# Making the x[128] rows of ten tiles once and loading them by DMA, and a block-diagonal S in the Fourier stage

## The chip, the cores and the metric

One NeuronCore of a Trainium2 chip runs the whole program. The metric is the device time of one execution in microseconds (us); times given are medians of several runs. Engines: TensorE (PE, matrix products, with PEld its weight loads), VectorE (DVE), ScalarE (ACT), GpSimd (POOL), and SyncE (SP), which here only issues DMAs.

## The reference

The input x is 2 x 3008 x 256, f32. It is Fourier transformed along the sequence and along the features, the real part is kept, and the 6016 tokens go through two feed-forward layers with 2048 hidden features:

```python
X = np.fft.fft(np.fft.fft(x, axis=1), axis=2).real        # 2 x 3008 x 256 -> 6016 x 256
h = X @ w_in;   y = (np.maximum(h, 0.0) ** 2) @ w_out      # first layer
h = y @ w_in2;  P = a0 + a1*h + a2*h*h + a3*h*h*h
Q = 1 + abs(b0)*abs(h) + abs(b1)*h*h
out = (P / (Q + 1e-6)) @ w_out2                            # second layer
```

## The kernel before, in words

**The transform.** 3008 = 64 x 47. A start-up part multiplies x by the length-47 matrix and leaves the result in the SBUF tile U. The rest is done per token tile: *D* (f_d, line 490) multiplies two units of U (128 columns) by the matrices of the feature transform, which leaves 2 x 129 columns in PSUM: a cosine part and a sine part of 64 + 64 features each, and in each part a last column for feature 128 (x[128]). *v* (f_v, line 498) copies that to SBUF on ACT. *S* (f_s, line 512) does the length-64 transform: v is the stationary operand, a constant of sines and cosines (rcs) the moving one. f_eh (line 528) rounds the result to the matmul format on ACT (the high part, tile x1h, and X0 with the rows for x[128]); f_el (line 544) makes the low part by a subtraction on DVE (line 547), and the low part of row 64 of X0 (line 549).

**One job** is D, v, S, f_eh and f_el for two units, that is 128 columns of the tile's transformed input. In v of before, each unit's cosine and sine halves have to end up on all 128 partitions, so there are four copies of 64 partitions x 129 (line 509; job 0 of tile 0 is special, with one copy, line 502). S then has four matmuls in a job: for each of the two units one with 128 moving columns (line 523) and one with 64 (line 524). The second one has feature 128 of v, broadcast to 128 stationary columns, so that every row of its result is x[128]; it goes to X0. All these are f32 matmuls, which the trace shows as two passes each, each pass with a weight load of its own.

**The layers.** There are 12 tiles: tile 0 has 3 units, the others 4 (two jobs each; 47 units and 24 jobs, of which job 0 of tile 0 is special). Tokens k and -k share their products: the first layer's matmuls (h1, lines 630 to 633 for the DIRECT tiles 0 and 1, lines 648 and 650 for the others) work on half of a tile's columns. Each product of f32 accuracy is three matmuls of high and low parts; the contribution of feature 128 is a seventh matmul with w0 as the weights and X0 as the moving operand (line 650; line 631 in the DIRECT tiles). w0 is zero but in rows 0, 32 and 64, which hold the high, low and high part of that row of w_in; X0's rows 0, 32 and 64 must hold x[128]'s high, high and low part. o1 and o2 (line 674) are the output matmuls of the layers, h2 (line 617) the second layer's input matmul; ACT, DVE and POOL do the polynomials between them. Layer 2 of a tile runs beside layer 1 of the next one, and the jobs of a tile beside layer 1 of the tile before it.

**The order.** No engine's order is written out. Every operation is entered with `add(key, engine, cost, place, fn, needs, take, give, ...)`: an estimated cost, a due place, what it needs, and which buffers it takes and gives back. Queues.run (line 63) goes through them as a list scheduler with a clock per engine: of everything that can start earliest it takes the one with the smallest place. The order found this way is the program order of every engine. So a changed cost or a dropped operation can change the order of others. Engines run their queues in order on the chip.

**Start-up.** The weights of both layers are 64-bit floats and are loaded, converted and split on ACT and DVE while tiles 0 and 1 run. The U units of tiles 2 to 11 are spilled to DRAM (udram) and read back per tile (fd). Between the jobs of tile 0, TensorE also runs two groups of six matmuls on a tile of zeros (`hot`, line 286) which nothing reads.

Of the kernel before, what the change touches and what calls it, by code (L numbers as in the profile page):

```python
# [9 lines left out]
F32 = mybir.dt.float32  # L10
# [26 lines left out]
LAG1, LAG2, M2_AT, M2_SPAN = 1.23, 4.02, 1.04, 15.75  # L37
F_AT, F_STEP, F_GAP, F_GAP0 = 1.05, 3.59, 2.15, 0.4
# [119 lines left out]
def body(ctx: ExitStack, tc: tile.TileContext, x0, xf, w1i, w1o, w2i, w2o, a_in, b_in,  # L158
# [14 lines left out]
    rcs = cd_t[:, 258:514].rearrange("p (u c n) -> p u c n", u=2, c=2)  # L173
# [3 lines left out]
    a0, a1, a2, b0 = (ab[:, i:i + 1] for i in (0, 1, 2, 4))  # L177
    udram = dr.tile([128, 2, 94 * 32], F32, name="udram")
# [95 lines left out]

    hot_t = stp.tile([128, 128], F32, name="hot_t")
# [234 lines left out]


    def f_s(t, k, tag):
        v = FU.pop((t, k, "v"))
        f = ps(tag, [128, 512])
        FU[t, k] = p, r = f[:, 0:256].rearrange("p (c n) -> p c n", c=2), f[:, 256:384]
        if t + k == 0:
            nc.tensor.matmul(p[:, 0, :], v[:, 0:128], r0c, start=True, stop=True)
            nc.tensor.matmul(p[:, 1, :], v[:, 129:257], r0s, start=True, stop=True)
            nc.tensor.matmul(r, v[:, 128:129].to_broadcast([66, 128]), r0c, start=True, stop=True)
        else:  # L520
            for u in range(2):
                cols = slice(u * 64, u * 64 + 64)
                nc.tensor.matmul(p[:, :, cols], v[:, u, 0:128], rcs[:, u], start=True, stop=True)
                nc.tensor.matmul(r[:, cols], v[:, u, 128:129].to_broadcast([128, 128]), rcs[:, u, 0], start=True, stop=True)

    def f_eh(t, k, i):
        if i == 0:
            X1[t] = [sb("x1" + part, [128, 2, NMAX // 2], F32R) for part in "hl"]  # L530
            X0[t] = sb("x0", [128, NMAX // 2], F32R)
# [3 lines left out]
        nc.scalar.activation(out=X0[t][:, cols], in_=r, func=ACTF.Copy)  # L535
# [8 lines left out]
    def f_el(t, k, i):  # L544
        cols = slice(i * 128, i * 128 + 128)
        p, r = FU.pop((t, k))
        nc.vector.tensor_tensor(out=X1[t][1][:, :, cols], in0=p, in1=f32(X1[t][0][:, :, cols]), op=ALU.subtract)
        x = X0[t][64:65, cols]
        nc.vector.tensor_tensor(out=x, in0=r[64:65], in1=f32(x), op=ALU.subtract)

    for t in range(T):
# [5 lines left out]
        for i, k in enumerate(jobs):  # L557
# [9 lines left out]
            single = t + k == 0  # L567
            for part in range(1 if single else 2):
                add(("fv", t, k, part), "ACT", act(258, True) if single else 2 * act(129, True), place,
                    lambda k=key, p=part: f_v(*k, p), needs=[("fm",) + key] + ([("fv", t, k, 0)] if part else []),  # L570
                    give=(ft if t == 0 else ft[0],) if part or single else (), lat=0.2)
            add(("fs",) + key, "PE", 2 * mm4(128) + 2 * mm4(64), place + gap,
                lambda k=key, g=st: f_s(*k, bank(g)), needs=[("fv", t, k, 0 if single else 1)], take=(st,), give=("v",), lat=0.2)
            add(("fe",) + key, "ACT", act(256, True) + act(128, True), place + gap, lambda k=key, i=i: f_eh(*k, i),
                needs=[("fs",) + key], take=("x1h", "x1l", "x0") if k == 0 else (), after=[("fe", t, 0)] if k else [])
            add(("ff",) + key, "DVE", dve(256) + dve(128), place + gap, lambda k=key, i=i: f_el(*k, i),
                needs=[("fe",) + key], give=(st if t == 0 else st[0],), lat=0.2)
# [7 lines left out]
        needs=[k for k in queues.by_key if k[0] == "spill"] + [k for k in queues.by_key if k[0] in ("fm", "fs") and k[1] < 2]  # L585
# [245 lines left out]
    for t, j in ORDER1:  # L831
        for first, gs in (GROUPS1[t][j],):
# [8 lines left out]
                needs=[k for k in queues.by_key if k[0] in ("ff", "fn") and k[1] == t] + ["w0"] + [("W", 1, i) for i in chunks],  # L841
# [84 lines left out]
def _consts():  # L926
# [99 lines left out]
```

## Time and profile before

| what | value |
|---|---|
| median of 3 runs | 1083.6 us (1082.31 to 1086.79) |
| profiled execution, its own time | 1083.8 us |
| its span in the trace | 1082.0 us |
| granted TensorE clock, mean over the span | 0.997 |
| PE / PEld busy | 1048.7 us (97%) / 987.8 us (91%) |
| DVE / ACT busy | 1008.0 us (93%) / 985.9 us (91%) |
| POOL busy | 488.8 us (45%) |

A row of instruction groups gives the source line, the engine, the operation, output <- input, shapes and count, then the busy time, the mean in ns of one, and the idle time before them. In a timeline, a row is one instruction or a run of equal ones: start, length, engine, line. A matmul's length is latency, and consecutive ones overlap: what one costs TensorE is read from the starts of its successors. A clock of 1.00 is 2.4 GHz; the other level is 1.2 GHz.

### The profile page before, as it was taken

What the parts mean: (1) busy time and instruction counts of PE and PEld (TensorE: products, weight loads), DVE (VectorE), ACT (ScalarE), POOL (GpSimd) and SP (SyncE); (2) the same over time, 40 slices, a digit from 0 to 9 for tenths busy, and PEclk for the clock granted to TensorE, in tenths of its full rate; (3) what the DMA queues carried; (4) which work ended last, traced back from release to release, by engine and by line L of the source; (5) the groups of instructions that cost most, each with busy time, mean ns of one, the idle gap of its engine ahead of it and who ended that gap; (6) DMA issues with size and microseconds to landing.
All of it is one profiled execution on the core that took longest, in us unless ns stands there. A gap on an engine that the chain in (4) does not pass through costs nothing.

```text
span 1082.0 us, 21256 instructions
## 1 busy us (share of the span) xinstructions
PE 1048.7 (97%) x7670; PEld 987.8 (91%) x7670; DVE 1008.0 (93%) x1808; ACT 985.9 (91%) x2008; POOL 488.8 (45%) x371
## 2 busy tenths in 40 slices
PE   9999989999999999999999999999999999999996
PEld 9899979899999999989899989999989999999885
DVE  6999999999899999999899899999899999889998
ACT  3888989999989999989999999999999999999997
POOL 0000025454454555445555545545545545545476
PEclk9999999999999999999999999999999999999989
DMA  9654400000000000000000000000000000000000
GB/s 337 205 205 128 137 1 2 25 1 11 10 12 11 11 11 11 2 20 11 2 21 11 1 21 11 2 21 12 1 21 10 2 11 11 2 11 11 1 11 20
DMA packets 26821, 36.81 MB, mean 34 GB/s; under 512 B 2299, under 2 KB 19325, under 8 KB 26717
## 3 DMA queue, kind: packets, MB, share of 16 engines
q1 hardware_dynamic: 26605, 35.07, 9.6%
q8 instruction: 61, 1.00, 0.4%
q14 instruction: 43, 0.35, 0.1%
q10 hardware_dynamic: 112, 0.39, 0.1%
HBM read 26.65 MB, written 8.78 MB: 33 GB/s over the span
## 4 chain that ended last, share of the span: by engine, by line
PE 43%; ACT 30%; DVE 17%; issue 6%; DMA 1%; POOL 1%; POOLq 0%; SPq 0%; ACTq 0%; DVEq 0%
PE o2a L674 11%; PE p L617 7%; PE o1a L674 5%; PE o1b L674 5%; ACT y L764 4%; PE p L648 4%; ACT t L741 3%; ACT g L703 3%; ACT y L768 3%; ACT g L709 3%; ACT u L751 3%; PE o2b L617 3%; DVE p L787 3%; ACT u L736 3%; DVE u L747 2%
## 5 line engine op out<-in xcount | busy, mean ns | idle before, releaser
L798 POOL TENSOR_TENSOR g<-t,y 128x512 fp32r<-128x512 f32 (+1 forms) x181 | 248.1, 1371 | 420.0 <-DVE t L794 334.5
L718 POOL TENSOR_TENSOR g<-g,g 128x512 fp32r<-128x512 f32 x160 | 211.2, 1320 | 153.5 <-ACT g L713 101.8
L674 PE MATMUL o2a<-g,w2hi 128*128 128x256 f32 (+1 forms) x1440 | 262.6, 283 | 7.9 <-POOL g L798 6.0
L674 PEld LDWEIGHTS o2a<-g,w2hi 128*128 128x128 f32 x1440 | 210.1, 189 | 15.5 <-POOL g L798 8.6
L781 DVE SCALAR_TENSOR_TENSOR g<-t,ab,y 128x512 fp32r<-128x512 f32 (+1 forms) x177 | 137.1, 776 | 11.7 <-ACT y L768 10.9
L674 PE MATMUL o2a<-g,w2lo 128*128 128x256 f32 (+1 forms) x720 | 144.6, 281 | 0.0
L674 PE MATMUL o1a<-g,w1hi 128*128 128x512 f32 x352 | 140.0, 398 | 1.5 <-POOL g L718 1.5
L674 PE MATMUL o1b<-g,w1hi 128*128 128x512 f32 x352 | 138.6, 394 | 0.0
L787 DVE SCALAR_TENSOR_TENSOR p<-u,g 128x512 f32<-128x512 f32 (+1 forms) x176 | 131.3, 746 | 0.7
L794 DVE SCALAR_TENSOR_TENSOR t<-t,ab,p 128x512 f32<-128x512 f32 (+1 forms) x177 | 128.5, 726 | 1.1
L751 ACT ACTIVATE u<-u 128x512 f32<-128x512 f32 (+1 forms) x176 | 109.5, 622 | 14.0 <-DVE u L747 13.3
L617 PE MATMUL p<-x2h,w2hi 128*128 128x256 f32 (+1 forms) x534 | 110.4, 288 | 8.2 <-DVE t L759 3.7
L768 ACT ACTIVATE y<-y 128x512 f32<-128x512 f32 (+1 forms) x185 | 115.3, 624 | 1.6
L764 ACT ACTIVATE y<-u 128x512 f32<-128x512 f32 (+1 forms) x176 | 109.1, 621 | 7.1 <-POOL g L798 3.5
L703 ACT ACTIVATE g<-g 128x512 f32<-128x512 f32 x160 | 101.2, 632 | 15.4 <-DVE g L693 15.1
L747 DVE SCALAR_TENSOR_TENSOR u<-u,ab,p 128x512 f32<-128x512 f32 (+1 forms) x133 | 96.5, 726 | 19.3 <-ACT t L741 18.0
L709 ACT ACTIVATE g<-g 128x512 fp32r<-128x512 f32 (+1 forms) x175 | 109.7, 627 | 3.3 <-PE o1b L674 1.9
L674 PEld LDWEIGHTS o2a<-g,w2lo 128*128 128x128 f32 x720 | 110.7, 189 | 0.0
L713 ACT ACTIVATE g<-g 128x512 f32<-128x512 f32 (+1 forms) x175 | 109.5, 626 | 1.2
L617 PE MATMUL p<-x2h,w2lo 128*128 128x256 f32 (+1 forms) x534 | 107.9, 284 | 0.0
L617 PE MATMUL p<-x2l,w2hi 128*128 128x256 f32 (+1 forms) x534 | 107.8, 284 | 0.0
L693 DVE TENSOR_TENSOR g<-p,bc 128x256 f32<-128x256 f32 x238 | 96.2, 415 | 5.6 <-ACT bc L683 2.3
(261 smaller groups left out, 2862.4 us busy)
## 6 DMA issues: line engine op xcount, KB each, us to landing
g<-in_dram SPq DMA_DIRECT2D x48, 256.0 KB, 3.1
xt<-in_dram SPq DMA_DIRECT2D x15, 384.0 KB, 5.6
out_dram<-os SPq DMA_DIRECT2D x22, 256.0 KB, 2.1
udram<-U SPq DMA_DIRECT2D x4, 640.0 KB, 5.2
ut<-udram SPq DMA_DIRECT2D x10, 256.0 KB, 3.1
x2h<-in_dram SPq DMA_DIRECT2D x8, 256.0 KB, 5.0
x2l<-in_dram SPq DMA_DIRECT2D x8, 256.0 KB, 4.3
xt<-in_dram ACTq DMA_DIRECT2D x1, 384.0 KB, 4.1
```

Source lines behind the costliest of these rows:

```text
L617: nc.tensor.matmul(h[:, c * n:(c + 1) * n], l[:, k, :], r[:, k], start=(q == 0), stop=(q == 5))
L674: nc.tensor.matmul(O[t][e], l[:, e * 128:(e + 1) * 128], r[:, c * n:(c + 1) * n], start=(i == 0 and q == 0 and (e == 0 or not one)), stop= ...
L703: nc.scalar.activation(out=e["g"], in_=e["g"], func=ACTF.Relu)
L709: nc.scalar.activation(out=e["gh"], in_=e["g"], func=ACTF.Square)
L718: eng.tensor_tensor(out=e["gl"], in0=e["g"], in1=f32(e["gh"]), op=ALU.subtract)
L751: nc.scalar.activation(out=w, in_=w, func=ACTF.Abs)
L764: nc.scalar.activation(out=e["z"], in_=e["w"], func=ACTF.Abs_reciprocal_sqrt, bias=Q1)
L768: nc.scalar.activation(out=z, in_=z, func=ACTF.Square)
L781: nc.vector.scalar_tensor_tensor(out=e["gh"], in0=e["t1"], scalar=a0, in1=e["z"], op0=ALU.add, op1=ALU.mult)
L787: nc.vector.scalar_tensor_tensor(out=e["m"], in0=e["w"], scalar=Q1, in1=f32(e["gh"]), op0=ALU.add, op1=ALU.mult)
L794: nc.vector.scalar_tensor_tensor(out=e["t1"], in0=e["t1"], scalar=a0, in1=e["m"], op0=ALU.add, op1=ALU.subtract)
L798: (nc.vector if (t, j) in FIN else nc.gpsimd).tensor_tensor(out=e["gl"], in0=e["t1"], in1=e["z"], op=ALU.mult)
```

## The change

- **S** of the jobs after the first: the moving constant `rcs` becomes two block-diagonal matrices (128 x 128 each: two units in one), so that v keeps the layout that D leaves. One copy of D's result per job does for the four; S has two matmuls of 128 moving columns. In the DIRECT tiles 0 and 1, S keeps a third matmul, of 128 columns, for x[128].
- **x[128] of tiles 2 to 11**: D leaves out its column there (128 moving columns for 130), S its matmuls, f_eh its second copy and f_el its second subtraction.
- **New, once, in start-up**: 20 matmuls with one moving column each (q_mm, one per pair of units, in four groups of five), one ACT copy of the 20 columns (q_copy), one 128-column matmul (q_s), a rounding on ACT (q_hi), a subtraction on DVE (q_lo), and two DMAs from SP to DRAM (q_out).
- **New, per tile from 2 on**: three DMAs from SP that read rows 0, 32 and 64 of X0 from DRAM (q_row). The first-layer matmuls of the tile need them. X0 is one of two constant buffers; the DMAs take the buffer when the first layer of the tile two before has given it back.
- **Removed**: the two `hot` groups of tile 0.

```diff
+Q_AT, Q_STEP = -11.5, 0.5
...
-        nc.tensor.matmul(v[:, :, 64:129], u[:, 0, :], ca, start=True, stop=True)
+        last = 65 if t in DIRECT else 64
+        nc.tensor.matmul(v[:, :, 64:64 + last], u[:, 0, :], ca[:, :, :last], start=True, stop=True)
...
-        a, b = part * 64, 64 - part * 64
-        for o, c in ((a, 0), (b, 129)):
-            nc.scalar.activation(out=v[o:o + 64, part, :], in_=p[a:a + 64, c:c + 129], func=ACTF.Copy)
+        v = FU[t, k, "v"] = sb("v", [128, 258])[:p.shape[0]]
+        if t not in DIRECT:
+            v, p = (x.rearrange("p (b n) -> p b n", b=2)[:, :, 0:128] for x in (v, p))
+        nc.scalar.activation(out=v, in_=p, func=ACTF.Copy)
...
-            for u in range(2):
-                cols = slice(u * 64, u * 64 + 64)
-                nc.tensor.matmul(p[:, :, cols], v[:, u, 0:128], rcs[:, u], start=True, stop=True)
-                nc.tensor.matmul(r[:, cols], v[:, u, 128:129].to_broadcast([128, 128]), rcs[:, u, 0], start=True, stop=True)
+        for c in range(2):
+            nc.tensor.matmul(p[:, c], v[:, c * 129:c * 129 + 128], rcs[:, c], start=True, stop=True)
+        if t in DIRECT:
+            nc.tensor.matmul(r, v[:, 128:129].to_broadcast([128, 128]), rcs[:, 0], start=True, stop=True)
...
-        nc.scalar.activation(out=X0[t][:, cols], in_=r, func=ACTF.Copy)
+        if t in DIRECT:
+            nc.scalar.activation(out=X0[t][:, cols], in_=r, func=ACTF.Copy)
...
+        if t not in DIRECT:
+            return
         x = X0[t][64:65, cols]
         nc.vector.tensor_tensor(out=x, in0=r[64:65], in1=f32(x), op=ALU.subtract)
...
+    def q_mm(i, n):
+        if i == 0:
+            QP["v"] = ps("p3", [128, 512])
+        for k in range(i, i + n):
+            u = sum(TILES[:2]) + 2 * k
+            nc.tensor.matmul(QP["v"][:, k:k + 1], Uf[:, 0, (u - 1) * 64:(u + 1) * 64], ca[:, 0, 64:65], start=True, stop=True)
+    def q_copy():
+        nc.scalar.activation(out=qs, in_=QP["v"][:, 0:20], func=ACTF.Copy)
+    def q_s():
+        QP["q"] = q = ps("p3", [128, 512])[0:20, 0:128]
+        nc.tensor.matmul(q, qs, rcs[:, 0], start=True, stop=True)
+    def q_hi():
+        nc.scalar.activation(out=qh, in_=QP["q"], func=ACTF.Copy)
+    def q_lo():
+        nc.vector.tensor_tensor(out=ql, in0=QP["q"], in1=f32(qh), op=ALU.subtract)
+    def q_row(t):
+        X0[t] = x0t[t % 2]
+        k = (unit0[t] - sum(TILES[:2])) // 2
+        for row, part in ((0, 0), (32, 0), (64, 1)):
+            nc.sync.dma_start(out=f32(X0[t][row:row + 1]), in_=qdram[part:part + 1, k:k + 2].rearrange("o j n -> o (j n)"))
+    def q_out():
+        for part, x in enumerate((qh, ql)):
+            nc.sync.dma_start(out=qdram[part], in_=f32(x))
+    for i in range(0, 20, 5):
+        add(("qm", i), "PE", 5 * 0.22, Q_AT + i / 5 * Q_STEP, lambda i=i: q_mm(i, 5), needs=U_ALL, take=() if i else ("p3",),
+            after=[("qm", i - 5)] if i else [("fv", 0, 0)], lat=0.2)
...
+    for t in range(2, T):
+        add(("q", t), "SP", 0.4, 16 * (t - 1) + F_AT - 6, lambda t=t: q_row(t), take=("x0",), needs=["qd"], lat=DMA_LAT,
+            after=[("q", t - 1)] if t > 2 else [("fe", 1, 0)])
...
-            if t == 0:
-                add(("hot",) + key, "PE", 0.222 * 6, place + gap + 0.1, lambda: hot(6, "p0"), take=("p0",), give=("p0",),
-                    needs=[("fm",) + key])
...
-                needs=[k for k in queues.by_key if k[0] in ("ff", "fn") and k[1] == t] + ["w0"] + [("W", 1, i) for i in chunks],
+                needs=[k for k in queues.by_key if k[0] in ("ff", "fn", "q") and k[1] == t] + ["w0"] + [("W", 1, i) for i in chunks],
...
     rc[32], rs[0], rs[32] = alt, alt, -1.0
-    cc, ss = np.concatenate([rc, 0 * rc], axis=1), np.concatenate([0 * rs, rs], axis=1)
-    rcs = np.concatenate([np.concatenate([cc, ss]), np.concatenate([ss, cc])], axis=1)
+    rcs = np.block([[rc, z2, rs, z2], [z2, rc, z2, rs]])
```

The costs that the planner is given follow: v is one operation with the cost of 256 or 258 elements in place of two, S two 128-column matmuls (three in the DIRECT tiles), f_eh and f_el without their 128-element parts outside the DIRECT tiles.

## Rows read from the trace of the kernel before

**Rows 1.** The page's first part: busy us (share of the span) x instructions.
```profile
PE 1048.7 (97%) x7670; PEld 987.8 (91%) x7670; DVE 1008.0 (93%) x1808; ACT 985.9 (91%) x2008; POOL 488.8 (45%) x371
```
**Rows 2.** Windows: length, busy of PE, PEld, DVE, ACT, POOL, clock, DMA share, GB/s.
```profile
81.00:108.00 27.00, 27.00 (x197) 25.95 (x196) 24.50 (x50) 22.41 (x46) 0.00 (x0) 1.00 0.41 128
...
900.00:1000.00 100.00, 100.00 (x739) 94.65 (x738) 92.19 (x162) 95.99 (x190) 52.91 (x41) 1.00 0.03 9
```
**Rows 3.** Timeline of TensorE: one S of tile 11 and what follows.
```profile
902.30 0.38 PE L523 MATMUL p<-cd_t,v 128*128 128x128 f32 x2
902.52 0.33 PE L524 MATMUL p<-cd_t,v 128*128 128x64 f32 x2
902.69 0.44 PE L523 MATMUL p<-cd_t,v 128*128 128x128 f32 x2
902.96 0.33 PE L524 MATMUL p<-cd_t,v 128*128 128x64 f32 x2
903.11 0.48 PE L617 MATMUL p<-x2h,w2hi 128*128 128x256 f32 x2
903.42 0.39 PE L617 MATMUL p<-x2h,w2lo 128*128 128x256 f32 x2
903.65 0.39 PE L617 MATMUL p<-x2l,w2hi 128*128 128x256 f32 x2
```
**Rows 4.** Timeline of TensorE: the D of the same job and what follows.
```profile
891.91 0.38 PE L494 MATMUL p<-cd_t,ut 128*128 128x130 f32 x2
892.13 0.39 PE L495 MATMUL p<-cd_t,ut 128*128 128x128 f32 x2
892.27 0.48 PE L617 MATMUL p<-x2h,w2hi 128*128 128x256 f32 x2
892.59 0.40 PE L617 MATMUL p<-x2h,w2lo 128*128 128x256 f32 x2
```
**Rows 5.** Groups by line and shape: the instructions of the jobs that change.
```profile
L509 ACT ACTIVATE v<-p 64x129 f32<-64x129 f32 x84 | 22.8, 272 | 1.0
...
L524 PE MATMUL p<-cd_t,v 128*128 128x64 f32 x92 | 15.3, 249 | 0.0
...
L534 ACT ACTIVATE x1h<-p 128x256 fp32r<-128x256 f32 x24 | 9.2, 384 | 0.1
...
L549 DVE TENSOR_TENSOR x<-p,x 1x128 fp32r<-1x128 f32 x24 | 6.9, 289 | 0.4
L535 ACT ACTIVATE x<-p 128x128 fp32r<-128x128 f32 x24 | 6.8, 285 | 0.0
```
**Rows 6.** Timeline of start-up: the hot groups, one S, the first h1 matmul.
```profile
36.13 1.60 PE L286 MATMUL p<-hot_t 128*128 128x128 f32 x12 [0.53 <-ACT v L509]
...
37.72 0.30 PEld L523 LDWEIGHTS p<-cd_t,v 128*128 128x128 f32 x2 [0.17 <-ACT v L509]
...
38.66 1.56 PE L286 MATMUL p<-hot_t 128*128 128x128 f32 x12
...
41.32 0.36 PE L630 MATMUL p<-x1h,w1hi 128*128 128x256 f32 x1
```
**Rows 7.** TensorE's waits from 220 to 900: us in total, times, longest.
```profile
PE p L617 <- DVE t L759: 1.9, 4, 0.6
...
PE p L648 <- ACT v L509: 1.1, 2, 0.5
```
**Rows 8.** The same view from 1000 us to the end.
```profile
PE p L617 <- DVE x1h L792: 3.6, 2, 2.0
```
**Rows 9.** Windows around those waits, columns as in rows 2.
```profile
1028.00:1032.00 4.00, 2.39 (x14) 2.12 (x14) 4.00 (x7) 2.69 (x6) 3.82 (x4) 0.58 0.00 0
1032.00:1036.00 4.00, 4.00 (x22) 4.00 (x22) 3.84 (x7) 3.54 (x7) 2.15 (x2) 0.57 0.01 4
```
**Rows 10.** Instructions that read X0: ns min/median/max, first to last start.
```profile
L650 PE MATMUL p<-x,w x119: 276/276/284, 154.9 to 1000.5; 128*128 128x256 f32 x119
```
**Rows 11.** DMA issues: out, in, count, KB each, median us to landing.
```profile
w<-cw SPq DMA_DIRECT2D x3, 8.0 KB, 7.1
```

More of the change, by code (lines that the diff above doesn't have):

```diff
@@ L177, in body @@
     a0, a1, a2, b0 = (ab[:, i:i + 1] for i in (0, 1, 2, 4))
+    x0t = [const.tile([128, NMAX // 2], F32R, name=f"x0{i}") for i in range(2)]
+    qdram = dr.tile([2, 20, 128], F32, name="qdram")
     udram = dr.tile([128, 2, 94 * 32], F32, name="udram")
@@ L273, in u_out @@
                                 op=ALU.subtract if part else ALU.add)
+    qs = stp.tile([128, 20], F32, name="qs")
+    qh, ql = (stp.tile([20, 128], F32R, name=nm) for nm in ("qh", "ql"))
     hot_t = stp.tile([128, 128], F32, name="hot_t")
@@ L547, in f_el @@
         nc.vector.tensor_tensor(out=X1[t][1][:, :, cols], in0=p, in1=f32(X1[t][0][:, :, cols]), op=ALU.subtract)
+        if t not in DIRECT:
+            return
         x = X0[t][64:65, cols]
         nc.vector.tensor_tensor(out=x, in0=r[64:65], in1=f32(x), op=ALU.subtract)
+    QP = {}
+    def q_mm(i, n):
[14 more added lines that the diff above has]
+    def q_row(t):
+        X0[t] = x0t[t % 2]
+        k = (unit0[t] - sum(TILES[:2])) // 2
[7 more added lines that the diff above has]
+            after=[("qm", i - 5)] if i else [("fv", 0, 0)], lat=0.2)
+    add("qc", "ACT", 0.2, Q_AT + 4 * Q_STEP, q_copy, needs=[("qm", 15)], give=("p3",), lat=0.2)
+    add("qs", "PE", mm4(128), Q_AT + 4 * Q_STEP + 0.5, q_s, needs=["qc"], take=("p3",), lat=0.2)
+    add("qh", "ACT", 0.2, Q_AT + 4 * Q_STEP + 0.5, q_hi, needs=["qs"])
+    add("ql", "DVE", 0.25, Q_AT + 4 * Q_STEP + 0.5, q_lo, needs=["qh"], give=("p3",))
+    add("qd", "SP", 0.2, Q_AT + 4 * Q_STEP + 0.5, q_out, needs=["ql"], lat=DMA_LAT)
+    for t in range(2, T):
+        add(("q", t), "SP", 0.4, 16 * (t - 1) + F_AT - 6, lambda t=t: q_row(t), take=("x0",), needs=["qd"], lat=DMA_LAT,
+            after=[("q", t - 1)] if t > 2 else [("fe", 1, 0)])
     for t in range(T):
@@ L566, in body @@
                 needs=[("fd", t)] if t > 1 else U_ALL, take=(ft, "v"), give=("ut",) if t > 1 and k == jobs[-1] else (), lat=0.2)
[L567 to L576, printed above, removed]
+            full = t in DIRECT
+            add(("fv",) + key, "ACT", act(258 if full else 256, True), place, lambda k=key: f_v(*k), needs=[("fm",) + key],
+                give=(ft if t == 0 else ft[0],), lat=0.2)
+            add(("fs",) + key, "PE", 2 * mm4(128) + mm4(128) * full, place + gap,
+                lambda k=key, g=st: f_s(*k, bank(g)), needs=[("fv", t, k)], take=(st,), give=("v",), lat=0.2)
+            add(("fe",) + key, "ACT", act(256, True) + act(128, True) * full, place + gap, lambda k=key, i=i: f_eh(*k, i),
+                needs=[("fs",) + key], take=("x1h", "x1l", "x0")[:3 if t in DIRECT else 2] if k == 0 else (), after=[("fe", t, 0)] if k else [])
+            add(("ff",) + key, "DVE", dve(256) + dve(128) * full, place + gap, lambda k=key, i=i: f_el(*k, i),
                 needs=[("fe",) + key], give=(st if t == 0 else st[0],), lat=0.2)
-            if t == 0:
-                add(("hot",) + key, "PE", 0.222 * 6, place + gap + 0.1, lambda: hot(6, "p0"), take=("p0",), give=("p0",),
-                    needs=[("fm",) + key])
             if t in DIRECT:
```

16 lines of the change are left out of this document (4 added, 12 removed).

## The prediction

> **What bounds the kernel now.** I read the busy shares first. TensorE stands at 97% of the span, VectorE at 93%, ScalarE at 91%, GpSimd at 45% [rows 1]: three engines that are nearly full, so shares alone do not say which of them a saving must come from. The windows do: in the late tiles TensorE is busy in all of 100 us at a clock of 1.00, while VectorE shows 92.19 and ScalarE 95.99 [rows 2]; already in start-up there is a stretch, 81 to 108 us, with TensorE at 27.00 of 27.00 and the other two at 24.50 and 22.41 [rows 2]. The list of waits agrees: from 220 to 900 us the largest single cause for which TensorE stood still cost it 1.9 us [rows 7]. From the first h1 at 41.32 us [rows 6] to the last layer-1 matmuls at about 1000 us [rows 10], then, what TensorE no longer has to do comes off the end, and what the other engines no longer have to do is mostly hidden behind it. After that the last tile's layer 2 runs out, with VectorE full (4.00 of 4 us) and TensorE waiting [rows 8, 9]; no part of the change lies there.
>
> **S, tiles 2 to 11: the main term.** A matmul's length is latency, so the price is read from starts. One S runs from 902.30; the second h2 pair behind it starts at 903.42; an h2 pair normally takes 903.65 - 903.42 = 0.23 us. So S occupies TensorE for 1.12 - 0.23 = 0.89 us [rows 3]. By the same reading D, with two matmuls of some 128 columns, takes 892.59 - 891.91 - 0.23 = 0.45 us [rows 4]. S has eight passes and D four: both come to 0.11 us a pass, although half of S's passes have only 64 columns. The pass is paid for its weight load and not for its columns. After the change S has exactly the shape of D, so a job saves 0.89 - 0.45 = 0.44 us. Most other jobs show the same starts to within 0.02 us, a few 0.08 more in S and in D alike. There are 46 halves in rows 5 (92 passes), that is 23 jobs, of which 20 belong to tiles 2 to 11: 20 x 0.44 = 8.8 us. For the lower end I let the second pair cost 0.27, as the one from 902.69 to 902.96 does: 0.50 for S, 7.8 us in all. D's two columns less change nothing by this reading.
>
> The Trainium skill, "TensorE: Matmul & The Clock Gate", section "Back-to-back issue gap", gives about 81 ns per load-and-matmul pair at 128 columns. By that the four passes saved would be 0.32 us a job, 6.5 us in all, and the forecast 2.3 us later. The trace does not agree: its starts give 0.11 us, and the trace decides.
>
> **S, tiles 0 and 1.** Three jobs go from eight passes to six (three matmuls of 128 columns): 3 x 2 x 0.11 = 0.66 us.
>
> **Start-up, where work is added.** Out go two hot groups of 12 passes, which at 0.11 are 1.32 us each, 2.64 together. In come 20 one-column matmuls, 40 passes. The trace has no pass of one column. Its nearest row is the 64-column one: 0.17 for two passes at the cheapest place (902.52 to 902.69), and 0.27 for the pair that follows it, that is 0.085 to 0.14 a pass [rows 3], so 3.4 to 5.6 us; since the load sets the price I take 0.11, 4.4 us. q_s is two passes more, 0.22. Against that, TensorE stood still there for 0.53 and 0.17 us until the copies of v were done [rows 6]. With one copy at the price of 256 elements (0.384) in place of four at 0.272 (1.09) [rows 5] each v is done 0.7 us sooner, and q_mm has nothing to wait for but U: I take these 0.7 us as filled. Net: 4.4 + 0.22 - 2.64 - 0.7 = +1.3 us at the first h1. Ends: 3.4 + 0.22 - 2.64 - 0.7 - 0.7 (the copy's gain passed on once more) = -0.4, and 5.6 + 0.22 - 2.64 = +3.2 with no gap filled. The full stretch of 81 to 108 us says that such a shift is not absorbed later.
>
> Behind q_copy and q_hi on ScalarE, and q_lo on VectorE, stand the weight conversion of layer 1 and the copies of tiles 0 and 1. Each of the three is priced by the smallest rows of its engine (0.28, 0.28 and 0.29, [rows 5]); on ScalarE the three jobs of tiles 0 and 1 give back 3 x (1.09 - 0.38) = 2.1 us in the same stretch, so I count nothing for them. If ScalarE stands at q_copy until the last of the 40 passes, it is the upper end above that pays for it.
>
> **The DMAs.** q_out is 2 issues on SP, q_row 30. The three small row writes that the kernel already has landed after 7.1 us [rows 11]. A tile's rows are issued once the first layer of the tile two before has given X0 back, and are needed when its own first layer starts, one tile in between: layer 1 of ten tiles runs from 154.9 to 1000.5 us [rows 10], 84.6 us a tile. The wait for a free buffer isn't new either, since f_eh of that tile waits for x1h, which the same h1 gives back. Behind q_row on SP stand, for the first tiles, weight loads of layer 2, and later the outputs and the reads of U, which come once a tile. Cost 0. If the cover of a tile were gone, 7.1 us would show as a wait before its first L650; if q_row waited in front of a weight load, as much at that load. I see nothing that brings either about, and leave both out of the sum and in the upper part of the range.
>
> **ScalarE and VectorE in tiles 2 to 11.** Per job four copies become one and the X0 copy goes: 1.09 - 0.38 + 0.285 = 0.99 us, 19.8 us in 20 jobs. VectorE loses 0.289 a job, 5.8 us. Beside a full TensorE these are worth only what they take out of its waits. The one wait that names v is 1.1 us in two places [rows 7]; D's bank is now given back after one copy instead of after two pairs. The order is planned anew, so such waits do not carry over one by one: I take half, -0.5, with ends 0 and -1.1.
>
> **Sum.** -8.8 - 0.66 + 1.3 - 0.5 = -8.7 us on the profiled execution: 1083.8 (span 1082.0, and 1.8 around it) becomes 1075.1. The median of the runs is 0.2 lower, so I predict 1075.0. Ends of the terms: -8.8 - 0.66 - 0.4 - 1.1 = -11.0 (1072.6) and -7.8 - 0.66 + 3.2 = -5.3 (1078.3). The new order itself I let do 3 us either way, about the two groups of rows 7 together.
>
> **Rivals.**
> - *VectorE sets the pace.* With 92 to 93% busy and small gaps between dependent instructions it may be nearer its limit than the share tells. Then the gain is its own: 5.8 less 0.29 for q_lo, 1083.6 - 5.5 = 1078.1. Against it: TensorE has no gaps in 900 to 1000 us, VectorE 7.8 us of them [rows 2]. Chance 0.14.
> - *TensorE's clock falls in start-up.* The hot groups go, and 40 passes move one column each. The trace shows the clock fall once after TensorE had waited (3.6 us in two waits around 1026 to 1032 us): 0.58 and 0.57 in two windows of 4 us, which lie between the levels of 1.2 and 2.4 GHz, so most of the stretch was at the lower one [rows 8, 9]. That took (0.42 + 0.43) x 4 = 3.4 us of TensorE's time. The same between 36 and 44 us gives 1078.4. For it: no row shows what one-column passes do to the clock. Against: TensorE does not stand still there. The Trainium skill, the same page, section "What's actually happening", has the gate follow how busy the array has been lately; by that the fall is possible without any wait. No row here shows it. Chance 0.13.
> - *The freed time becomes waits.* The loop of h2, polynomial and o2 goes through all four engines; if its latency sets the pace, S's 8.8 us turn into idle time before L617 and L674, and only start-up's +1.3 - 0.66 stay: 1084.2. Against it: next to no waits of TensorE between 900 and 1000 us. Chance 0.11.
> - *Slower than before.* The new order makes TensorE wait at the seam between tiles, long enough for the clock to fall, as after 1026 us. One such place costs 3.6 us of waits and 3.4 of clock, 7.0 [rows 8, 9]. One leaves 1082; from two places on the gain is used up: 1075.0 + 14.0 = 1089.0. For it: every cost of the jobs has changed, and the order with it. Against: the old order has eleven seams and one such place, in the last, where no layer 1 is left to fill. Chance 0.08.
>
> **How the numbers follow.** The forecast keeps 0.54. The range of 8 in 10 is 1069.5 to 1082.5: the ends of the terms with 3 us of order on both sides (the upper end, with the two middle rivals inside, reaches 1 us further); outside are the last two rivals, 0.19. A measurement of this kernel tells no less than about 0.5% (5.4 us) from no change, so faster means under 1078.2. Forecast: 0.47 of its 0.54 lie there, and about half of the first two rivals, 0.14: 0.61. Slower than 1089.0 is half of the last rival and some of the third's tail, 0.07. The rest, 0.32, is no change.
>
> **What would show it.** S of a late tile: two rows of two passes, 0.68 us from the first to the second start behind it. No 64-partition copies, 20 copies of 128x256 of about 0.38 us in their place, and 4 one-row subtractions for 24. The first h1 at about 42.6 us, at a clock of 1.00 from 33 to 48. The 40 new passes at 0.11 us. The last S of tile 11 starts about 7 to 8 us earlier than 902.30, and the stretch behind it is as long as before. No wait before L650 on a DMA. The prediction is wrong if S has shrunk as told and the seams hold the difference as waits, if the clock column is under 1.00 in start-up, or if TensorE's busy time falls by some 8 us and the last tile's run-out is longer by as much.

## The result

| | before | changed |
|---|---|---|
| median of 6 runs each | 1083.44 us (1082.31 to 1086.79) | 1075.53 us (1070.95 to 1078.99) |
| profiled execution (span) | 1083.8 us (1082.0) | 1074.8 us (1073.0) |
| ratio | | 0.9917, 95% interval 0.9889 to 0.9946 |

1075.0 was predicted. The sum came out; three of its parts did not, and two of them cancel. First the changed kernel's page, its first part and its chain of waits:

```profile
PE 1042.3 (97%) x7602; PEld 985.1 (92%) x7602; DVE 999.5 (93%) x1789; ACT 957.8 (89%) x1921; POOL 488.6 (46%) x371
...
PE 65%; DVE 17%; ACT 12%; issue 4%; POOL 1%; DVEq 0%; POOLq 0%; ACTq 0%
```

and the chain of the kernel before, which the prediction had not used:

```profile
PE 43%; ACT 30%; DVE 17%; issue 6%; DMA 1%; POOL 1%; POOLq 0%; SPq 0%; ACTq 0%; DVEq 0%
```

Beside [rows 1], TensorE is as full as it was, and ScalarE lost 28 us. The chain, which runs through whatever released the next piece of work, went through ScalarE for 30% of the span before and does for 12% after.

**S is what it was said to be.** Timeline of TensorE, last S of tile 11, changed kernel (compare [rows 3]):

```profile
893.16 0.39 PE L715 MATMUL o1b<-g,w1hi 128*128 128x512 f32 x1
893.39 0.60 PE L522 MATMUL p<-cd_t,v 128*128 128x128 f32 x4
893.76 0.48 PE L658 MATMUL o2b<-x2h,w2hi 128*128 128x256 f32 x2
894.08 0.39 PE L658 MATMUL o2b<-x2h,w2lo 128*128 128x256 f32 x2
```

From 893.39 to the second start behind it 0.69 us, less an h2 pair of 0.23: 0.46 where it was 0.89. It starts 8.9 us earlier than in [rows 3]. The groups by line and shape show the one-column passes and 15 of the 20 copies of tiles 2 to 11; the others are in a group of their own (compare [rows 5]):

```profile
L560 PE MATMUL p<-cd_t,U 128*128 128x1 f32 x40 | 6.6, 295 | 0.0
...
L509 ACT ACTIVATE v<-p 128x256 f32<-128x256 f32 x15 | 5.8, 387 | 0.2 <-PE p L501 0.2
```

**Start-up is not.** Timeline of TensorE in the changed kernel (compare [rows 6]), then windows with their clock in the last column but two:

```profile
35.05 2.29 PE L560 MATMUL p<-cd_t,U 128*128 128x1 f32 x20
...
37.20 0.83 PE L522 MATMUL p<-cd_t,v 128*128 128x128 f32 x4
37.83 0.64 PE L524 MATMUL p<-cd_t,v 128*128 128x128 f32 x2
38.25 4.27 PE L560 MATMUL p<-cd_t,U 128*128 128x1 f32 x20
...
43.24 0.56 PE L671 MATMUL p<-x1h,w1hi 128*128 128x256 f32 x1
```
```profile
33.00:36.00 3.00, 2.98 (x24) 2.61 (x24) 2.96 (x9) 2.80 (x8) 0.00 (x0) 1.00 1.00 316
36.00:39.00 3.00, 3.00 (x23) 3.00 (x23) 2.90 (x9) 1.53 (x6) 0.00 (x0) 0.77 0.88 293
39.00:42.00 3.00, 3.00 (x16) 3.00 (x16) 2.55 (x8) 1.42 (x5) 0.00 (x0) 0.50 0.64 204
42.00:45.00 3.00, 3.00 (x16) 3.00 (x16) 2.27 (x5) 1.18 (x4) 0.00 (x0) 0.50 0.00 0
45.00:48.00 3.00, 3.00 (x15) 2.48 (x14) 0.52 (x3) 1.44 (x4) 0.00 (x0) 0.50 0.45 141
48.00:51.00 3.00, 3.00 (x16) 3.00 (x16) 1.44 (x4) 1.47 (x5) 0.00 (x0) 0.50 0.61 181
51.00:54.00 3.00, 3.00 (x24) 3.00 (x24) 2.94 (x7) 2.68 (x7) 0.00 (x0) 0.96 0.11 40
```

The first 20 one-column passes take (37.20 - 35.05) / 20 = 0.11 us each, the last 20 take (42.38 - 38.25) / 20 = 0.21, where 42.38 is the start of the D that follows them. Between the two, near 37.7 us, the granted clock falls from 1.00 to 0.50, the 1.2 GHz level, without TensorE having waited since 33.0 us, and it stays there until about 51 us. VectorE and ScalarE then wait for it: 0.52 and 1.44 of 3 us in the window from 45 us. The first h1 comes at 43.24 us.

The rest of the run is read from one mark, the copy of a tile's finished layer 1 into x2h on ScalarE (timelines of ScalarE, tiles 3 and 11; first before, then changed):

```profile
341.90 0.60 ACT L724 ACTIVATE x2h<-o1a 128x512 fp32r<-128x512 f32 x1
...
1011.26 0.58 ACT L724 ACTIVATE x2h<-o1a 128x512 fp32r<-128x512 f32 x1
```
```profile
347.69 0.63 ACT L765 ACTIVATE x2h<-o1a 128x512 fp32r<-128x512 f32 x1
...
1001.56 0.58 ACT L765 ACTIVATE x2h<-o1a 128x512 fp32r<-128x512 f32 x1
```

Up to tile 3 the changed kernel is 5.8 us late. From tile 3 to tile 11 it needs 653.9 us where 669.4 were needed, 15.5 less. Behind that 71.4 for 70.7, 0.7 more. Together -9.0. The prediction had about -2 (1.3 for start-up, less 0.66, less six jobs of S at 0.44), -6.5 (14 jobs of S, and part of the waits) and 0.

Windows from 300 to 1000 us, before and changed, show how much of those 15.5 us had looked like idle time of TensorE:

```profile
300.00:1000.00 700.00, 693.53 (x5160) 654.76 (x5159) 658.92 (x1126) 661.23 (x1327) 361.28 (x269) 1.00 0.03 10
```
```profile
300.00:1000.00 700.00, 697.75 (x5215) 660.44 (x5215) 665.27 (x1136) 658.63 (x1303) 369.43 (x276) 1.00 0.03 10
```

TensorE was busy in 99.1% of the window before, and still does 55 instructions more in the same time after. It stood still for 6.5 us of the 700 before and for 2.3 after, so some 4 of the 15.5 us were idle time that could be seen; the rest came out of its busy row.

### The profile page after: what moved, and what is told of

It is laid out like the page before. It is cut to its first block, busy times and chain, and to the rows that moved or that the text cites. A ratio compares the mean times of both kernels' runs of the same rounds, so it can differ in the third digit from the quotient of the medians.

```text
span 1073.0 us, 21023 instructions
## 1 busy us (share of the span) xinstructions
PE 1042.3 (97%) x7602; PEld 985.1 (92%) x7602; DVE 999.5 (93%) x1789; ACT 957.8 (89%) x1921; POOL 488.6 (46%) x371
## 4 chain that ended last, share of the span: by engine, by line
PE 65%; DVE 17%; ACT 12%; issue 4%; POOL 1%; DVEq 0%; POOLq 0%; ACTq 0%
PE o2a L715 17%; PE p L658 11%; PE o1a L715 8%; PE o1b L715 8%; PE p L689 7%; PE o2b L658 5%; DVE g L822 2%; DVE t L796 2%; DVE p L828 2%; DVE t L800 2%; PE o2b L689 2%; DVE u L788 2%; DVE t L835 1%; ACT g L750 1%; ACT t L782 1%
## 5 line engine op out<-in xcount | busy, mean ns | idle before, releaser
L715 PEld LDWEIGHTS o2a<-g,w2hi 128*128 128x128 f32 x1440 | 209.1, 190 | 13.3 <-POOL g L839 8.7
L822 DVE SCALAR_TENSOR_TENSOR g<-t,ab,y 128x512 fp32r<-128x512 f32 (+1 forms) x177 | 134.7, 761 | 3.5 <-ACT y L809 2.4
L828 DVE SCALAR_TENSOR_TENSOR p<-u,g 128x512 f32<-128x512 f32 (+1 forms) x176 | 135.3, 769 | 0.2
L734 DVE TENSOR_TENSOR g<-p,bc 128x256 f32<-128x256 f32 x266 | 107.2, 416 | 6.8 <-POOL g L759 5.7
L658 PE MATMUL p<-x2h,w2hi 128*128 128x256 f32 (+1 forms) x514 | 104.7, 285 | 7.7 <-DVE x1h L833 3.7
L788 DVE SCALAR_TENSOR_TENSOR u<-u,ab,p 128x512 f32<-128x512 f32 (+1 forms) x128 | 92.9, 726 | 20.6 <-ACT t L782 20.5
L658 PE MATMUL p<-x2h,w2lo 128*128 128x256 f32 (+1 forms) x514 | 102.9, 282 | 0.0
L658 PE MATMUL p<-x2l,w2hi 128*128 128x256 f32 (+1 forms) x514 | 102.7, 281 | 0.0
```

Source lines behind the costliest of these rows:

```text
L658: nc.tensor.matmul(h[:, c * n:(c + 1) * n], l[:, k, :], r[:, k], start=(q == 0), stop=(q == 5))
L715: nc.tensor.matmul(O[t][e], l[:, e * 128:(e + 1) * 128], r[:, c * n:(c + 1) * n], start=(i == 0 and q == 0 and (e == 0 or not one)), stop= ...
L788: nc.vector.scalar_tensor_tensor(out=e["w"], in0=w, scalar=b0, in1=H2[t, j], op0=ALU.add, op1=ALU.mult)
L822: nc.vector.scalar_tensor_tensor(out=e["gh"], in0=e["t1"], scalar=a0, in1=e["z"], op0=ALU.add, op1=ALU.mult)
L828: nc.vector.scalar_tensor_tensor(out=e["m"], in0=e["w"], scalar=Q1, in1=f32(e["gh"]), op0=ALU.add, op1=ALU.mult)
```

## The experiments

Two questions: what lets the clock fall in start-up and what it costs, and where the 15.5 us come from. All ratios are to the kernel before, which ran beside each kernel, with medians of 1083.7 to 1084.3 us. A profile is of one execution of each kernel.

### 65 columns for one, in the same order

```diff
-        for k in range(i, i + n):
+        for k in range(19 - i, 19 - i - n, -1):
             u = sum(TILES[:2]) + 2 * k
-            nc.tensor.matmul(QP["v"][:, k:k + 1], Uf[:, 0, (u - 1) * 64:(u + 1) * 64], ca[:, 0, 64:65], start=True, stop=True)
+            nc.tensor.matmul(QP["v"][:, k:k + 65], Uf[:, 0, (u - 1) * 64:(u + 1) * 64], ca[:, 0, 0:65], start=True, stop=True)
...
-        nc.scalar.activation(out=qs, in_=QP["v"][:, 0:20], func=ACTF.Copy)
+        nc.scalar.activation(out=qs, in_=QP["v"][:, 64:84], func=ACTF.Copy)
```

> The changed kernel with one edit: the 20 matmuls of q_mm move 65 columns instead of 1 (they go from the last to the first, so that each leaves its own x[128] column standing). The order of every engine is the same, and so is the number of passes and weight loads. Theory A (the one-column passes starve the array and let the clock fall): the clock is 1.00 from 36 to 54 us where the changed kernel shows 0.50 to 0.77, the first h1 starts at about 41.5 us instead of 43.2, and the run takes about 1070 us, some 5 us less than the changed kernel. Theory B (the clock falls because the two hot groups are gone): the clock falls to 0.50 as before and the time stays at about 1075.5. Theory C (the clock does not matter, the lost time is made up later): the clock is 1.00 and the time still 1074 to 1076.

Measured: 1068.75 us, ratio 0.9856 (0.9836 to 0.9876), 6.8 us under the changed kernel with the order of every engine the same. Timeline of TensorE and windows:

```profile
34.77 2.34 PE L560 MATMUL p<-cd_t,U 128*128 128x65 f32 x20
...
37.68 2.35 PE L560 MATMUL p<-cd_t,U 128*128 128x65 f32 x20
...
40.28 0.36 PE L671 MATMUL p<-x1h,w1hi 128*128 128x256 f32 x1
```
```profile
36.00:39.00 3.00, 3.00 (x30) 3.00 (x28) 2.90 (x9) 1.66 (x7) 0.00 (x0) 1.00 0.85 287
39.00:42.00 3.00, 3.00 (x28) 2.94 (x26) 2.53 (x8) 2.03 (x7) 0.00 (x0) 1.00 0.53 170
...
51.00:54.00 3.00, 2.05 (x16) 1.86 (x15) 2.90 (x10) 2.35 (x9) 0.00 (x0) 1.00 0.41 139
54.00:57.00 3.00, 1.48 (x7) 0.77 (x5) 2.91 (x8) 1.83 (x7) 0.00 (x0) 0.98 0.59 211
57.00:60.00 3.00, 2.99 (x15) 2.99 (x15) 2.93 (x8) 1.42 (x5) 0.00 (x0) 0.50 0.00 0
```

Theory A: both blocks run at 0.11 us a pass, the clock stays at 1.00, the first h1 comes at 40.28, even 1 us sooner than before. More than that 1 us is work moved and not saved: before, one S and one D of tile 1, 1.3 us by their starts, stand ahead of the first h1 at 41.32; in the new order they come behind it, at 49.34 and 51.06. Timeline of TensorE before:

```profile
40.05 0.39 PE L523 MATMUL p<-cd_t,v 128*128 128x128 f32 x2
...
40.90 0.44 PE L494 MATMUL p<-cd_t,U 128*128 128x130 f32 x2
```

With 65 columns moving the passes cost the same and hold the clock; with one column they do not. The time is 1.3 us below A's. TensorE then waits between 51 and 57 us, 0.9 us for v from ScalarE and 1.5 for x1l from VectorE, which is nearly full there (2.90 and 2.91 of 3 us), and the clock falls once after that wait. B and C fall.

### The hot groups back

```diff
+            if t == 0:
+                add(("hot",) + key, "PE", 0.222 * 6, place + gap + 0.1, lambda: hot(6, "p0"), take=("p0",), give=("p0",),
+                    needs=[("fm",) + key])
```

> The changed kernel with the two hot groups of tile 0 put back (six 128-column matmuls on zeros each, 12 passes); the planner sees them, so the order changes. Theory A (one-column passes starve the array): the clock still falls behind the first block of one-column passes, and the time is 1075 to 1078 (2.6 us of passes more). Theory B (the hot groups hold the clock): the clock is 1.00 from 36 to 54 us and the time about 1072 to 1073.

Measured: 1076.15 us, ratio 0.9936 (0.9906 to 0.9966). The planner put a hot group into the first half of q_mm and one into the second. Timeline of TensorE:

```profile
34.78 1.18 PE L560 MATMUL p<-cd_t,U 128*128 128x1 f32 x10
35.82 1.59 PE L291 MATMUL p<-hot_t 128*128 128x128 f32 x12
37.24 1.18 PE L560 MATMUL p<-cd_t,U 128*128 128x1 f32 x10
...
39.03 1.18 PE L560 MATMUL p<-cd_t,U 128*128 128x1 f32 x10
40.06 2.28 PE L291 MATMUL p<-hot_t 128*128 128x128 f32 x12
42.14 2.13 PE L560 MATMUL p<-cd_t,U 128*128 128x1 f32 x10
```

Three of four one-column blocks run at 0.11 us a pass; then the clock falls inside the hot group itself (12 passes in 2.08 us), later than without, but it falls. In this execution the hot groups do not hold the clock, as theory A has it. But the ten runs lie in two groups of five: 1071.55 to 1073.63 us at a mean clock of 0.992 to 0.996, and 1078.67 to 1083.32 at 0.984 to 0.987. The profile is of the second group. The first has the time of theory B, and whether its clock fell in start-up no trace shows.

### q_mm later, between wide matmuls, without and with the hot groups

```diff
-Q_AT, Q_STEP = -11.5, 0.5
+Q_AT, Q_STEP = 4.5, 1.0
...
-            after=[("qm", i - 5)] if i else [("fv", 0, 0)], lat=0.2)
+            after=[("h1", 0, 3 + i // 5)] + ([("qm", i - 5)] if i else []), lat=0.2)
```

> The changed kernel with q_mm moved: its four groups of five wait for the 4th to 7th layer-1 products of tile 0, so they run singly between wide matmuls, and the start-up up to the first h1 has neither q_mm nor hot groups. Theory A: the clock is 1.00 wherever TensorE is busy, the first h1 starts at 39 to 40 us, the time is 1069 to 1071. Theory B: the clock falls between 36 and 41 us for want of the hot groups, and the time is 1074 to 1076.

> As the kernel with q_mm moved behind the first products of layer 1, and with the two hot groups back. Theory A and B alike: the clock is 1.00, the first h1 at about 41 us, the time 1070 to 1072; by A it is no faster than the one without hot groups, by B some 4 us faster than that.

Measured: 1064.83 us, ratio 0.9814 (0.9796 to 0.9832), without hot groups, and 1072.62, ratio 0.9892 (0.9875 to 0.9909), with them. Timeline of TensorE and windows of the first:

```profile
38.20 0.36 PE L671 MATMUL p<-x1h,w1hi 128*128 128x256 f32 x1
```
```profile
36.00:39.00 3.00, 2.65 (x23) 2.68 (x24) 2.81 (x8) 2.70 (x13) 0.00 (x0) 1.00 0.98 347
39.00:42.00 3.00, 2.42 (x22) 2.28 (x21) 2.91 (x9) 2.22 (x6) 0.00 (x0) 1.00 0.51 159
```

Without q_mm and without hot groups the first h1 comes 3.1 us sooner than in [rows 6], and the clock holds although TensorE is busy in only 2.42 of 3 us. So the hot groups were not needed here, and B falls; the time is 4 us below the lower end of A. That the version with them is 7.8 us slower was expected by neither theory. Its profiled execution is 5.2 us longer: 4.1 arise before tile 3, where TensorE waits between 51 and 57 us and the clock falls, as above; 4.9 between tiles 3 and 11, where the work is the same and only the order differs; behind that 3.7 come back (table below).

### 65 columns in the late version

> The kernel with q_mm behind the 4th to 7th products of layer 1, and with 65 columns instead of 1 as well, in the same order as the one-column version of it. By theory A the one-column passes do no harm in blocks of ten between wide matmuls, so the time is the same, 1064 to 1066. If they still cost clock there (the late part of start-up showed 0.72 to 0.90 around 141 to 159 us), it is 2 to 4 us less.

The edit is that of the first experiment on top of the later q_mm. Measured: 1063.99 us, ratio 0.9818 (0.9801 to 0.9834), no different from 1064.83: in blocks of ten passes between wide matmuls one column does no harm. These two are the fastest versions, 19 to 20 us under the kernel before and 11 under the changed one.

### Work put back into TensorE, ScalarE and VectorE, one at a time

All four start from the 65-column version and keep the order of every engine. The edits, in this sequence: S twice; three copies of v and one more row subtraction; three copies of v alone; the subtraction alone.

```diff
-        for c in range(2):
+        for c in (0, 1) if t in DIRECT else (0, 1, 0, 1):
```
```diff
-        nc.scalar.activation(out=v, in_=p, func=ACTF.Copy)
+        for _ in range(1 if t in DIRECT else 3):
+            nc.scalar.activation(out=v, in_=p, func=ACTF.Copy)
...
         if t not in DIRECT:
+            nc.vector.tensor_tensor(out=X1[t][1][64:65, 0, cols], in0=p[64:65, 0], in1=f32(X1[t][0][64:65, 0, cols]), op=ALU.subtract)
             return
```

> The kernel with 65-column q_mm, in the same order, and each S of tiles 2 to 11 issues its two matmuls twice: 4 passes more in 20 jobs, as many as the change took out of S. If TensorE paces the tiles (theory P) the time rises by 20 x 0.44 = 8.8 us, from 1068.8 to 1077.5. If another engine or the latency of the loop paces them (theory L), it rises by less than 3 us, to 1071 at most.

> The kernel with 65-column q_mm, in the same order, with the relief of ScalarE and VectorE undone in tiles 2 to 11: each copy of v is made three times (0.77 us more a job) and a one-row subtraction of 128 columns is added in f_el (0.29 us). Between the tile seams of the middle of the run the changed kernel gained about 1.9 us a tile, of which S explains 0.88. If the rest comes from the relief of the two engines (theory R), the time rises by 7 to 10 us, to 1076 to 1079. If it comes from the new order (theory O), the rise is under 2 us, to 1069 to 1071.

> The kernel with 65-column q_mm, in the same order, with only the copies of v made three times in tiles 2 to 11 (0.77 us of ScalarE a job, 15.4 us in all). With the one-row subtraction on VectorE as well the time rose by 13.3 us. Theory R-A (ScalarE's relief is what the tiles gain by): 1077 to 1081. Theory R-D (VectorE's is): 1069 to 1071. If each engine's time costs what it takes, in proportion (0.77 to 0.29): about 1078.

> The kernel with 65-column q_mm, in the same order, with only a one-row subtraction of 128 columns added in f_el of tiles 2 to 11 (0.29 us of VectorE a job, 5.8 us in all). Theory R-D: 1076 to 1080. Theory R-A: 1069 to 1071. In proportion: about 1073.

| put back in 20 jobs | its own time | median | ratio (interval) | cost | mean clock of the runs | cost from tile 3 to 11, of its own time there |
|---|---|---|---|---|---|---|
| nothing | | 1068.75 | 0.9856 (0.9836 to 0.9876) | | 0.996 | |
| 80 passes on TensorE | 8.8 us | 1074.31 | 0.9907 (0.9891 to 0.9924) | 5.6 | 0.999 | 5.5 of 6.2 |
| copies and subtractions | 15.4 + 5.8 | 1082.06 | 0.9982 (0.9972 to 0.9993) | 13.3 | 0.997 | 7.9 of 14.8 |
| copies on ScalarE | 15.4 | 1078.05 | 0.9940 (0.9923 to 0.9956) | 9.3 | 0.998 | 6.0 of 10.8 |
| subtractions on VectorE | 5.8 | 1073.00 | 0.9887 (0.9871 to 0.9904) | 4.3 | 0.995 | 0.7 of 4.1 |

The medians hold falls of the clock that the kernels do not share. All five wait alike for 2.5 us between 51 and 57 us; in the profiled executions the clock then falls in three (0.50 in the window from 57 to 60 us with nothing put back, 0.60 with the copies and 0.60 with the subtractions) and stays at 1.00 in two (the passes; copies and subtractions together). Between tiles 3 and 11 (marks below) no kernel here has a clock under 1.00, so the last column is the cleaner price, though from one execution each.

By it TensorE's passes cost nearly what they take: by the median theory P got 5.6 of its 8.8 us, but at a mean clock 0.003 higher, which over 1070 us is some 3 us (an estimate). ScalarE's copies, which the prediction had priced at next to nothing, cost 56% of themselves there and 60% by the median, so R-A holds beside P; with the subtractions the rise was 13.3 us, more than the 7 to 10 of R. The price of VectorE's subtractions stays open: 4.3 us by the median, 0.7 in the stretch, with more falls of the clock in its profile. No engine alone sets the pace. TensorE's windows, nothing put back and with the copies alone, show where most of the copies' cost goes:

```profile
300.00:1000.00 700.00, 697.73 (x5212) 660.28 (x5211) 664.38 (x1135) 657.71 (x1300) 369.07 (x275) 1.00 0.03 10
```
```profile
300.00:1000.00 700.00, 693.43 (x5164) 654.64 (x5163) 659.25 (x1126) 661.56 (x1318) 366.93 (x273) 1.00 0.03 10
```

TensorE stands still for 2.3 us of the 700 without the copies and for 6.6 with them.

### The same from the other side: only the planner's costs, and only ScalarE's relief

```diff
-                add(("fv", t, k, part), "ACT", act(258, True) if single else 2 * act(129, True), place,
+                add(("fv", t, k, part), "ACT", act(258, True) if single else act(258 if t in DIRECT else 256, True) / 2, place,
...
-            add(("fs",) + key, "PE", 2 * mm4(128) + 2 * mm4(64), place + gap,
+            add(("fs",) + key, "PE", 2 * mm4(128) + mm4(128) * (t in DIRECT), place + gap,
```

(and the costs of f_eh and f_el in the same way)

> The kernel before with all its instructions, where only the costs that the planner is told for the jobs are those of the changed kernel (one copy for v in two halves, two matmuls for S, no x[128] part in tiles 2 to 11). So the order changes in about the way it did, and no work goes. Theory R (relief): 1083 to 1085. Theory O (order): 1075 to 1077, with the late tiles about 1 us shorter each.

```diff
+        if t not in DIRECT: nc.scalar.activation(out=v[:, part, :], in_=p[:, part * 129:part * 129 + 129], func=ACTF.Copy)
         for o, c in ((a, 0), (b, 129)):
-            nc.scalar.activation(out=v[o:o + 64, part, :], in_=p[a:a + 64, c:c + 129], func=ACTF.Copy)
+            if t in DIRECT: nc.scalar.activation(out=v[o:o + 64, part, :], in_=p[a:a + 64, c:c + 129], func=ACTF.Copy)
```

> The kernel before, in its own order, with two copies of 128 x 129 in place of the four of 64 x 129 for each v of tiles 2 to 11 (so v has the wrong halves there; all other work is as before). That takes some 0.54 us of ScalarE out of each of 20 jobs, 10.9 us in all, and nothing out of TensorE or VectorE. If ScalarE's time costs 55 to 60% of itself, as the copies that were added showed (theory R-A): 1083.8 - 6 = 1078. If ScalarE's relief is worth next to nothing beside a full TensorE, as the prediction had it: 1083 to 1084.

Measured: costs only 1083.95 us, ratio 0.9994 (0.9985 to 1.0004): this new plan alone gives nothing, which speaks against theory O; it is not the very order of the changed kernel. Two copies fewer per job, in the old plan: 1073.93, ratio 0.9916 (0.9897 to 0.9934), 9.7 us for 10.9 us of ScalarE, with not one instruction less on TensorE (v has wrong halves there, which changes values and not work). Its chain of waits, its window and its two marks on ScalarE:

```profile
PE 71%; DVE 12%; ACT 11%; issue 3%; DMA 1%; POOL 1%; POOLq 0%; ACTq 0%; DVEq 0%; SPq 0%
```
```profile
300.00:1000.00 700.00, 697.37 (x5211) 660.73 (x5210) 662.06 (x1137) 659.40 (x1311) 367.72 (x272) 1.00 0.03 10
```
```profile
337.71 0.60 ACT L725 ACTIVATE x2h<-o1a 128x512 fp32r<-128x512 f32 x1
...
1001.06 0.58 ACT L725 ACTIVATE x2h<-o1a 128x512 fp32r<-128x512 f32 x1
```

TensorE stands still for 2.6 us of the 700 where it was 6.5, and ScalarE's share of the chain falls from 30 to 11%, as in the changed kernel. The kernel with three copies of v has it at 19%:

```profile
PE 56%; DVE 19%; ACT 19%; issue 5%; POOL 1%; DVEq 0%; POOLq 0%; ACTq 0%
```

That share is a rough guide: it is also 19% in the version with the hot groups back, whose stretch from tile 3 to 11 is that of the changed kernel (12%) to 0.1 us:

```profile
PE 59%; ACT 19%; DVE 16%; issue 5%; POOL 1%; POOLq 0%; DVEq 0%; ACTq 0%
```

### S and the copy alone

```diff
-        last = 65 if t in DIRECT else 64
+        last = 65
...
-        if t in DIRECT:
+        if True:
             nc.tensor.matmul(r, v[:, 128:129].to_broadcast([128, 128]), rcs[:, 0], start=True, stop=True)
...
-    for i in range(0, 20, 5):
-        add(("qm", i), "PE", 5 * 0.22, Q_AT + i / 5 * Q_STEP, lambda i=i: q_mm(i, 5), needs=U_ALL, take=() if i else ("p3",),
...
```

(and with it the other q operations go, f_eh and f_el keep their x[128] parts in all tiles, the hot groups stay)

> One half of the change alone: block-diagonal S and one copy of v in all jobs; x[128] stays in S as a third matmul of 128 columns in all tiles, with its copy and its subtraction, the hot groups stay, and there is no q_mm, no q DMA. S goes from eight passes to six in 23 jobs, 5.1 us; ScalarE loses 0.70 us a job. Theory P with S's own term only: 1078.5. With the waits that the whole change lost (about 1 us a tile, by relief of ScalarE or by the new order) on top: 1069 to 1072. The clock stays at 1.00 up to 54 us.

Measured: 1074.15 us, ratio 0.9904 (0.9888 to 0.9921), between the two values. Half of the change gives as much as the whole did; the whole with 65 columns in q_mm gives 5.4 us more.

### The marks of all kernels

Start of the x2h copies of tiles 3 and 11 in the profiled execution of each kernel, the stretch between them, and from there to the end of the span, us. The 14 jobs of tiles 5 to 11 lie in the stretch.

```
kernel                       tile 3  tile 11  stretch   rest
before                       341.90  1011.26   669.36   70.7
changed                      347.69  1001.56   653.87   71.4
65 columns                   343.02   997.44   654.42   69.8
  + 80 passes                342.62  1002.56   659.94   69.2
  + copies                   346.54  1006.95   660.41   71.4
  + subtractions             344.52   999.63   655.11   72.9
  + copies, subtractions     347.35  1009.65   662.30   71.4
hot back                     351.95  1005.88   653.93   71.0
late q_mm                    339.23   994.15   654.92   70.9
late q_mm, hot               343.37  1003.14   659.77   67.2
late q_mm, 65 columns        336.38   991.16   654.78   69.6
costs only                   346.15  1015.18   669.03   67.3
two copies fewer (before)    337.71  1001.06   663.35   70.5
S and copy alone             335.47  1001.59   666.12   69.2
```

## Why the prediction was right, point by point

- **What bounds the kernel: wrong.** The step read TensorE's fullness as the bound and everything else as hidden. With 14 x 0.54 = 7.6 us less on ScalarE and the same TensorE work the stretch shrank by 6.0 us; with 14 x 0.44 = 6.2 us more on TensorE it grew by 5.5. Both engines were on the path. Of the 6.0 us, 3.8 were idle time of TensorE that could be seen (6.5 us of 700, then 2.6); the rest lay inside its busy row, which is made of latencies that overlap. The Trainium skill, "Perfetto Trace Analysis", section "Identifying the Most-Contended Engine", says that the busy share of matmuls is not a good measure of how close TensorE is to its limit, and names the share of peak arithmetic and the busy share of the weight loads instead; the trace agrees as far as the loads go: 99.1% against 93.5% (654.76 of 700 us) in the window of before, and 94.3% after.
- **S in tiles 2 to 11, 0.44 us a job: right as a price.** S takes 0.46 us for 0.89. As a term of the sum it was a little large: 80 passes put back cost 5.5 of 6.2 us from tile 3 to 11; the 5.6 of 8.8 by the medians are at unequal clocks.
- **ScalarE's and VectorE's relief, -0.5: wrong, the largest miss.** The step took half of the one wait that names v, 1.1 us. TensorE's idle time from all causes was 6.5 us of the 700, and fell to 2.6 with nothing but fewer copies of v: beside the waits for v, those of h2 for t on VectorE (1.5 us) went too. In the stretch: of the 15.5 us, TensorE's share is 5.5 by the passes put back. The copies put back cost 6.0 us for 14 x 0.77 = 10.8, the copies left out gave 6.0 for 7.6, that is 0.56 to 0.79 of ScalarE's own time. At the 14 x 0.99 = 13.9 us of the change this is 7.8 to 11.0, and the subtractions add 0.7. The sum, 14.0 to 17.2, holds the 15.5. This is worked out from single profiled executions, and the orders of the two kernels differ, which alone was worth 4.9 us in another pair; so a share of the order is not excluded.
- **Start-up, +1.3: wrong, through the rival that had a chance of 0.13.** The clock fell, under the one-column passes. Its price was put at 3.4 us; by the same-order comparison it is 6.8 us of the median, and 4.7 us at the mark of tile 3 in the profiles. With the clock held, the first h1 came 1.0 us sooner than before, where 1.3 later was said. Most of that difference is order: one S, one D and q_s, which the step had ahead of the first h1, now come behind it. The waits for v are gone, as the step had it. The rule cited there, that the gate follows how busy the array has been ("TensorE: Matmul & The Clock Gate" of the Trainium skill, "What's actually happening"), allowed a fall without a wait, and in the 4 us before this one there was none; but the busy row stood at 3.00 of 3 us, so that row does not show what the gate follows.
- **One-column passes at 0.11 us: right** while the clock held (20 at 0.11, with one column or 65), 0.21 after it.
- **DMAs at nothing: right.** The row loads appear in no wait of TensorE; late q_mm moves them too, without cost.
- **The slower rival and the waits at the seams: did not happen.** The stretch behind tile 11 is within 0.7 us.

So the sum was right by cancellation, which is luck: up to tile 3 the kernel was 5.8 us late where about 2 early was said, 4.7 us of that the clock, and from tile 3 to 11 it gained 15.5 us where 6.5 was said. The prediction had itself named a clock under 1.00 in start-up as a sign that it is wrong, and that sign came. The runs of the changed kernel show the clock's part; its six, sorted by time (in the profiled one, of 1074.79 us, the clock falls again in the run-out, to 0.77 in the window from 1060 to 1063 us):

```
us       1070.95  1071.84  1074.79  1076.26  1076.29  1078.99
clock      0.994    0.993    0.990    0.988    0.988    0.985
```

**Open.** Up to tile 3 the 65-column version is 1.1 us later than before, although six jobs got cheaper. Its own fall of the clock after 57 us can be part of that: the version with 80 passes put back, which has none, is there 0.4 us sooner in spite of 24 passes more. VectorE is nearly full there, but no run took anything from it. The same work in another order (late q_mm with and without hot groups) differs by 4.9 us in the stretch, and S and the copy alone gained only 3.2 us there for 0.70 us of ScalarE a job, less than the others would give. How much of each version's stretch is order and how much relief is settled only where the order was held.

## What to carry to other kernels

Where three engines stand above 90%, the busy shares and a window with TensorE at 100% do not say which one pays. Add up all the idle time of the fullest engine, not one named wait (6.5 us here, against 1.1), and count on some more inside its row. An engine with 30% of the chain of waits was worth relieving, but the chain is rough: 12 to 19% in kernels with the same stretch. Price such relief by taking a little work out of one engine, or putting some in, with the order held, and compare stretches in which the clock is even. Weight loads with next to nothing to move behind them cost the full pass and can cost the clock as well: move more columns, or spread them between wide matmuls.

## What the runs showed of the hardware

- Two f32 matmul streams with the same 40 weight loads at the same pace (0.11 us a pass): with 1 moving column the granted clock fell to 0.50 near 37.7 us, though TensorE had not waited since 33.0 us; with 65, behind the same wait, it stayed at 1.00 through the same stretch.
- A clock that has fallen need not come back soon under full work: TensorE was busy in 3.00 of 3 us in each window from 39 to 51 us, at 0.50, the last 8 us of them behind the one-column passes.
- The same waits need not end alike: after 2.5 us of them between 51 and 57 us, at most 1.5 at a time, the clock fell in three of five profiled executions with the same order.
- f32 passes cost 0.11 us with 1, 65 or 128 moving columns, and the passes of S before, half with 64 and half with 128, came to 0.11 in the mean: at a clock of 1.00 the columns did not set the price.
- ScalarE copies of 64 x 129 and of 128 x 129 take 273 and 279 ns, so half the partitions saved nothing.
